# Numerators in like tiles, scaling one product later, and LayerNorm and weight parts moved, in an attention and MLP block

## The chip, the cores and the metric

The kernel runs on one core of a Trainium2 chip. The metric is the device time of one execution in microseconds (us). TensorE (PE, with its weight loads shown as PEld), VectorE (DVE), ScalarE (ACT), GpSimd (POOL) and SyncE (SP, which here only issues DMAs) each work through a queue of their own in order, and wait for one another by semaphores.

## The reference

A transformer block for 2048 tokens of width 640 with 32 heads of 20, all in fp32:

```
h = layernorm(x) * (1 + ca) + sa
pq, pk = per-head linear map of q and k
phi = concat(softmax(p), softmax(-p))        # for q and for k
kv  = phi_k^T v ;  z = sum over tokens of phi_k
o   = (phi_q kv) / (phi_q z + 1e-6)
x   = x + ga * (o @ wo)
h   = layernorm(x) * (1 + cb) + sb
x   = x + gb * (relu(h @ w1 + b1)^2 @ w2 + b2)
```

The six rows sa to gb come from silu(c) @ w_mod. The hidden width of the MLP is 1728.

## The kernel before

Precision: a large product is made of three fp32r products (high x high, high x low, low x high). A matrix is therefore kept as a high part, rounded to fp32r, and a low part, the rest. Small products are left in fp32, which TensorE does in two passes.

The work has three stages. The first (to about 262 us) makes k, v and q for 16 tiles of 128 tokens, the two softmaxes, and the sum kv over all tokens. The exponentials of q, "e", go to DRAM for tiles 0 to 11 and stay in SBUF for tiles 12 to 15. The second stage (about 262 to 409 us) is the one that the diff touches: it turns e into the output of the attention and multiplies by wo. The third is the MLP: a loop over eight blocks j of 256 tokens and seven steps n, with `up` (h @ w1) and `down` (@ w2).

The second stage, per tile t:

- `load_e(t)` (L772) brings e back from DRAM; its SBUF buffer must have been released by an earlier tile's scaling.
- `e_prod(t)` (L784): DVE multiplies e by z (L788) and sums over each head (L790). POOL then makes three small steps (L792, L794, L795), which give the denominator dd.
- `e_recip(t)` (L797): DVE takes the reciprocal (L801) and multiplies it by the softmax sums (L802), on DVE or POOL depending on the tile.
- `e_scale(t)` (L804): DVE scales e by that factor into one of four buffers "ezb" (L809 and a small piece, L814).

Per block j of two tiles: `tr_e(j)` (L820) transposes the scaled e on TensorE ("te", L829), and ACT copies it out (L831). `num(j)` (L835) makes the numerators: for five groups of six heads two products of 64 columns each, and for the last two heads one product with kv5, which holds their 40 columns three times side by side, so that the result has three copies on 120 partitions. The three tiles of the result are "numa", "numb" and "numc". `num_hi(j)` (L855): ACT rounds them to the high parts. `num_lo(j)` (L860): TensorE subtracts the high parts from the numerators by a product with minus the identity ("neg", L864), and ACT copies the rest out as low parts (L866). For the last two heads the 120 partitions end up as low, high, high against high, high, low rows of wo, so that one product does the work of three. `do_wo(j, i, h, a, b)` (L870) makes products a to b of the 16 that multiply tile i of the block by column part h (384 or 256 columns) of wo ("pwo"), and ACT copies the result out ("at", L884).

The loop over j runs from L1030; its body is an order written out by hand for PE, DVE, ACT and POOL. Iteration j multiplies block j by wo, transposes and makes the numerators of block j + 1, and does products and scalings for tiles b = 2j + 5, c = 2j + 6 and b - 1. SP is not part of the order by hand: its DMAs are placed by the framework's own planner. Within the loop also lie:

- `q_chain(t, False)` (the spread: maximum, minimum and two subtractions on DVE, L401 to L404), `exps` (two exponentials on ACT, L407 and L408) and `q_sums` (DVE, L449) for tiles 13, 14 and 15, whose softmax was left for later.
- `add_x` (L973) and `ln_parts` (L314) for block 0 of the MLP: the residual, then in three parts two sums, two squares and two scalings on ACT.
- `p_load`, `p_hi`, `p_lo` (L937 on): the next weight part of w1 or w2 is loaded, rounded by ACT to its high part (L916), and DVE makes its low part (L88). There are 28 parts in a fixed list. What is not made in the loop is made in the MLP, by `prep(4)` (one batch of four parts per step n of block 0; `PREPS`).

Of the kernel before, what the change touches and what calls it, by code (L numbers as in the profile page):

```python
# [11 lines left out]
AF = mybir.ActivationFunctionType  # L12
# [3 lines left out]
P = 128  # L16
# [35 lines left out]
def kernel(  # L52
# [23 lines left out]
    def mm(o, terms, first=True, last=True, skip=False):  # L76
        for i, (a, b) in enumerate(terms):
            nc.tensor.matmul(  # L78
                o, a, b,
                start=first and i == 0, stop=last and i == len(terms) - 1,  # L80
                skip_group_check=skip,
            )
# [323 lines left out]
    def exps(e):  # L406
        nc.scalar.activation(e[:, 0], e[:, 0], AF.Exp)  # L407
        nc.scalar.activation(e[:, 1], e[:, 1], AF.Exp, scale=-1.0)  # L408
# [363 lines left out]
    def load_e(t):  # L772
        if t >= KEPT:
            if t < NT:
                ET[t] = EQ[t]
            return
        ET[t] = tok2(("k", "k", f"x{t // 3 % 2}")[t % 3], f"el{t}")
        nc.sync.dma_start(flat(ET[t]), ESP[t])
# [5 lines left out]
    def e_prod(t):  # L784
        if t >= NT:
            return
        z = SCR[t % 2]
        nc.vector.tensor_tensor(z, flat(ET[t]), flat(zb), op=ALU.mult)  # L788
        dn = DN[t] = small([P, 2, H], "dn", f"dn{t}", 3)
        nc.vector.tensor_reduce(dn.rearrange("p s h -> p (s h)"), heads(z), axis=AX.X, op=ALU.add)  # L790
        rs = rs_q[:, t].rearrange("p (s h) -> p s h", s=2)
        nc.gpsimd.tensor_tensor(dn, dn, rs, op=ALU.mult)  # L792
        dd = DD[t] = small([P, H], "dd", f"dd{t}")
        nc.gpsimd.tensor_tensor(dd, dn[:, 0], dn[:, 1], op=ALU.add)  # L794
        nc.gpsimd.tensor_scalar(dd, dd, 1e-6, None, op0=ALU.add)  # L795

    def e_recip(t):  # L797
        if t >= NT:
            return
        rs = rs_q[:, t].rearrange("p (s h) -> p s h", s=2)  # L800
        nc.vector.reciprocal(DD[t], DD[t])  # L801
        (nc.vector if t < 6 or t == NT - 1 else nc.gpsimd).tensor_tensor(DN[t], rs, DD[t][:, None, :].to_broadcast([P, 2, H]), op=ALU.mult)  # L802

    def e_scale(t):  # L804
        if t >= NT:
            return
        dn = DN[t]
        EU[t] = EZB[t % 4]
        nc.vector.tensor_tensor(  # L809
            EU[t][:, :1200].rearrange("p (u s h d) -> p s u h d", s=2, h=3, d=DH),  # L810
            ET[t][:, :, :600].rearrange("p s (u h d) -> p s u h d", h=3, d=DH),
            dn[:, :, :30].rearrange("p s (u h) -> p s u h", h=3)[:, :, :, :, None].to_broadcast([P, 2, 10, 3, DH]), op=ALU.mult
        )
        nc.vector.tensor_tensor(  # L814
            EU[t][:, 1200:].rearrange("p (s h d) -> p s h d", s=2, d=DH),
            ET[t][:, :, 600:].rearrange("p s (h d) -> p s h d", d=DH),
            dn[:, :, 30:, None].to_broadcast([P, 2, 2, DH]), op=ALU.mult
        )
# [16 lines left out]
    def num(j):  # L835
        OT[j] = ht(f"ot{j}", j)
        ps = [bank(f"numa{j}"), bank(f"numb{j}"), tp(f"numc{j}")]
        for g in range(5):
            for c in range(2):
                mm(ps[g // 2][64 * c : 64 * c + 64, (g % 2) * 256 : (g % 2) * 256 + 256],  # L840
                   [(kvd[:, g, 64 * c : 64 * c + 64], EPT[j, g][:120, c])], first=(g % 2 == 0), last=False, skip=True)
        mm(ps[2][:120, 256:], [(kv5, EPT[j, 5][:80, 0])], first=False, last=False, skip=True)
        NUM[j] = ps
        OT[j, 5] = row("s3", f"ot5_{j}")[:, 80:336].bitcast(F32R)

# [2 lines left out]
    def num_parts(j):  # L848
        ps, parts = NUM[j], []
        for b, g in ((0, 2), (1, 2), (2, 1)):  # L850
            t = OT[j][:, 2 * b : 2 * b + g]
            parts.append((ps[b][:, : 256 * g].rearrange("p (g n) -> p g n", n=256), t[:, :, 0], t[:, :, 1]))
        return parts + [(ps[2][:120, 256:], OT[j, 5][:120], OT[j, 5][:120])]

    def num_hi(j):  # L855
        for b, (src, hi, _) in enumerate(num_parts(j)):
            r = GR[5][1] if b == 3 else P
            nc.scalar.activation(hi[:r], src[:r], AF.Copy)

    def num_lo(j):  # L860

        for b, (src, hi, low) in enumerate(num_parts(j)):
            r = GR[5][1] if b == 3 else P
            nc.tensor.matmul(src[:r], neg[:r, :r], hi[:r], start=False, stop=True, skip_group_check=True)  # L864
        for src, _, low in num_parts(j):
            nc.scalar.activation(low, src, AF.Copy)  # L866

    PWO, AT = {}, {}

    def do_wo(j, i, h, a=0, b=16):  # L870
        t = 2 * j + i
        if h == 0 and a == 0:
            PWO[t] = pj(f"pwo{t}")
            AT[t] = row("s2", f"at{t}")
        s = slice(i * P, (i + 1) * P)
        cs_, n = slice(*CUT[h]), CUT[h][1] - CUT[h][0]
        terms = []
        for g in range(5):
            w, o = WO[g], OT[j]
            terms += three(o[:, g, 0, s], o[:, g, 1, s], w[:, 0, cs_], w[:, 1, cs_])  # L880
        terms.append((OT[j, 5][:120, s], WO[5][:120, 0, cs_]))
        mm(PWO[t][h][:, :n], terms[a:b], first=(a == 0), last=(b == 16))
        if b == 16:
            nc.scalar.activation(AT[t][:, cs_], PWO[t][h][:, :n], AF.Copy)  # L884
            if h:
                nc.scalar.dma_start(A1[t], AT[t])
# [50 lines left out]
    def p_load(n=1):  # L937
        for _ in range(n):
            if todo["load"]:
                k, f = todo["load"].pop(0)  # L940
                prep_load(k, f, places[k, f](f"w{k}_{f}"))

    def p_hi(n=1):
        for _ in range(n):
            if todo["hi"]:
                prep_hi(*todo["hi"].pop(0))
# [69 lines left out]
    num(0)  # L1016
    num_hi(0)
    num_lo(0)
    e_recip(2)
    e_scale(2)  # L1020
    e_prod(3)
    e_recip(3)
    e_scale(3)
    e_prod(4)
    e_recip(4)
    load_e(5)
    load_e(6)
    SPREAD, SUMS = {1: 1, 3: 2}, {2: 1, 4: 2}
    ln0 = None
    for j in range(NB):  # L1030
        nxt = j + 1 < NB
        b, c = 2 * j + 5, 2 * j + 6
        late_te = j == 0
        te_at = (0, 1) if 0 < j < 6 else (1, 2)
        if j == 4:
            load_x1(0)
        if j < 5:
            p_load()
        if j == 5:
            q_chain(KEPT + 3, False)  # L1040
            e_scale(b - 1)
        else:
            e_prod(b)
            e_scale(b - 1)
            e_recip(b)
        load_e(b + 2)
        def te(at):
            for i, gs in enumerate((range(3), range(3, NG))):
                if nxt and not late_te and te_at[i] == at:
                    tr_e(j + 1, gs)  # L1050

        do_wo(j, 0, 0)
        te(0)
        do_wo(j, 0, 1)
        if j == 7:
            t2(0, 0)
            t2(0, 1)
        te(1)
        if j in SUMS:
            q_sums(KEPT + SUMS[j])  # L1060
        if j == 5:
            exps(EQ[KEPT + 3])
            q_sums(KEPT + 3)
            e_prod(b)
            e_recip(b)
        if j == 0:
            e_scale(b)
        e_prod(c)
        if j in SPREAD:
            q_chain(KEPT + SPREAD[j], False)  # L1070
        do_wo(j, 1, 0)
        if j == 7:
            t2(0, 2)
            t2(0, 3)
        te(2)
        if j == 6:
            next(ln0)
        if nxt:
            if late_te:
                tr_e(j + 1, range(NG))  # L1080
            num(j + 1)
            num_hi(j + 1)
        if j == 6:
            next(ln0)
        do_wo(j, 1, 1, 0, 8)
        if j == 7:
            t2(0, 4)
        if not nxt:
            do_wo(j, 1, 1, 8, 16)
        if nxt:  # L1090
            do_wo(j, 1, 1, 8, 11)
            num_lo(j + 1)
            do_wo(j, 1, 1, 11, 16)
        if j in SPREAD:
            exps(EQ[KEPT + SPREAD[j]])
        if j:
            e_scale(b)
        e_recip(c)
        load_e(c + 2)
        if j == 5:  # L1100
            add_x(0, 0, 1)
            ln0 = ln_parts(XM[0], "b0")
        if j == 6:
            next(ln0)
        if 1 <= j < 6:
            p_hi()
        if j == 5:
            p_load(2)
        if j == 6:
            p_hi(2)  # L1110
            p_lo(4)
            p_load(3)
        if j == 7:
            p_lo(3)
            p_load(2)
    order.__exit__(None, None, None)

# [447 lines left out]
```

## Time and profile before

| what | value |
|---|---|
| median of 3 runs | 801.46 us (798.03 to 801.79) |
| the profiled execution | 800.36 us, of which the span from first to last instruction is 798.7 us |
| PE, PEld, DVE, ACT, POOL busy | 98%, 94%, 73%, 56%, 16% of the span |
| attention stage, 262 to 409 us | PE busy 145.89 of 147 us, DVE 102.09, ACT 83.83, POOL 34.71 |
| HBM traffic over the span | 157 GB/s |

In a row of the timeline stand the start and the duration in us, the engine, the line, the operation, output <- input, the shape (rows x columns of the TensorE tile, then the moving data) and the count; in brackets the idle time of the engine ahead of it and what ended it. A row of several instructions lasts from the first one's start to the last one's end. In a row of waits stand the waiting engine and operation, what it waited for, and us in total, times, and the longest. In a row of groups stand busy us and mean ns of one, then idle us ahead of them. In a row of windows stand for PE, PEld, DVE, ACT and POOL busy us and instructions, then the granted TensorE clock, the share of the DMA engines and GB/s. "issue" is time in which the engine waited for nothing that the profile shows. TensorE's matmuls overlap: a matmul's duration reaches to the end of its pipeline, so the step from one to the next is shorter than its duration.

### The profile page before, as it was taken

Reading aid. Unit: us, or ns where it says so; the run is one execution under the profiler, and the core shown is the slowest. Engines: PE = TensorE matmul, PEld = TensorE weight load, DVE = VectorE, ACT = ScalarE, POOL = GpSimd, SP = SyncE. Lnnn points to the kernel's source line nnn. Section 1 sums busy time; section 2 is a strip of 40 time slices with the busy share of each in tenths; the row PEclk is TensorE's granted clock in tenths of the full one; section 3 lists DMA queues with packets and bytes.
Section 4 is the critical chain, followed back from the end, with each engine's and each line's share of the span. In section 5 each row is a group of like instructions: output and inputs, shape, how many; then the busy total and the mean of one; then the engine's idle time right before and its main releaser. Section 6 shows DMA issues by size and latency. Waiting matters only on the chain.

```text
span 798.7 us, 15281 instructions
## 1 busy us (share of the span) xinstructions
PE 785.4 (98%) x5983; PEld 750.5 (94%) x5983; DVE 579.3 (73%) x1046; ACT 443.3 (56%) x988; POOL 128.3 (16%) x259
## 2 busy tenths in 40 slices
PE   9999999999999999999999999998999999999997
PEld 8899999999999878898899999998999999999997
DVE  4499889998788688993546666775757667675756
ACT  4667675576753355565777737555364645536431
POOL 3001021010000114331000000131131313213110
PEclk9999999999999999999999999999999999999999
DMA  9713326423120243321347355996575967667450
GB/s 341 279 35 128 115 83 203 148 85 116 67 100 1 82 167 132 116 83 67 116 144 239 130 180 213 284 317 207 160 237 154 278 170 234 200 175 218 122 168 34
DMA packets 50560, 126.30 MB, mean 158 GB/s; under 512 B 5872, under 2 KB 6640, under 8 KB 50488
## 3 DMA queue, kind: packets, MB, share of 16 engines
q1 hardware_dynamic: 33432, 84.32, 31.0%
q0 software_dynamic: 14752, 35.76, 16.3%
q10 hardware_dynamic: 2304, 5.24, 1.7%
q8 instruction: 47, 0.77, 0.4%
q14 instruction: 25, 0.20, 0.1%
HBM read 95.32 MB, written 29.88 MB: 157 GB/s over the span
## 4 chain that ended last, share of the span: by engine, by line
PE 75%; DVE 10%; ACT 6%; issue 4%; POOL 3%; DMA 2%; POOLq 0%; ACTq 0%; DVEq 0%
PE up L78 18%; PE acc L78 14%; PE pk L78 8%; PE pq L78 7%; PE pv L78 7%; PE pwo L78 7%; PE acc3x L78 4%; PE kvp L421 2%; DVE dn L790 2%; DVE scr L788 2%; PE te L829 2%; DMA ring_b<-td_b 1%; PE ta L340 1%; PE tb L340 1%; DVE ezb L809 1%
## 5 line engine op out<-in xcount | busy, mean ns | idle before, releaser
L78 PE MATMUL up<-h,w 128*128 128x256 f32 x1640 | 208.7, 279 | 0.4 <-ACT ft L1149 0.4
L78 PEld LDWEIGHTS up<-h,w 128*128 128x128 f32 x1640 | 197.9, 189 | 1.1 <-ACT ft L1149 0.8
L1149 ACT ACTIVATE ft<-up,b_t 128x256 f32<-128x256 f32 x104 | 49.0, 472 | 106.6 <-PE up L78 106.1
L78 PE MATMUL acc<-w,ra 128*128 128x384 f32 x452 | 100.4, 338 | 0.4
L78 PE MATMUL pwo<-wo,ot 128*128 128x256 f32 (+3 forms) x512 | 83.2, 315 | 0.1
L1150 DVE TENSOR_TENSOR ft<-ft 128x256 f32<-128x256 f32 x104 | 44.0, 423 | 50.5 <-ACT ft L1149 48.8
L78 PE MATMUL pk<-wk,hT 128*128 128x384 f32 (+1 forms) x480 | 77.1, 312 | 0.9 <-ACT hT L352 0.9
L78 PEld LDWEIGHTS pwo<-wo,ot 128*128 128x128 f32 (+1 forms) x512 | 75.7, 188 | 1.9 <-ACT ot L866 0.4
L78 PEld LDWEIGHTS acc<-w,ra 128*128 128x128 f32 x452 | 72.7, 188 | 3.7 <-DVE ra L88 2.0
L78 PE MATMUL pq<-wq,hT 128*128 128x384 f32 (+1 forms) x480 | 74.9, 311 | 0.4 <-ACT k L397 0.4
L78 PE MATMUL pv<-wv,hT 128*128 128x384 f32 (+1 forms) x480 | 75.2, 309 | 0.0
L78 PEld LDWEIGHTS pk<-wk,hT 128*128 128x128 f32 x480 | 71.6, 188 | 2.7 <-ACT hT L352 1.1
L78 PEld LDWEIGHTS pq<-wq,hT 128*128 128x128 f32 x480 | 70.5, 188 | 1.5 <-ACT k L397 0.9
L78 PEld LDWEIGHTS pv<-wv,hT 128*128 128x128 f32 x480 | 70.5, 188 | 0.4
L88 DVE TENSOR_TENSOR ra<-ft,ra 128x384 fp32r<-128x384 f32 (+2 forms) x86 | 36.8, 449 | 34.3 <-ACT ra L1173 21.0
L88 DVE TENSOR_TENSOR h<-hfb,h 128x256 fp32r<-128x256 f32 x40 | 17.0, 425 | 46.4 <-ACT h L352 46.3
L1173 ACT ACTIVATE ra<-ft 128x384 fp32r<-128x384 f32 x48 | 25.2, 526 | 32.6 <-DVE ft L1150 25.2
L78 PE MATMUL acc3x<-w,ra 128*128 128x256 f32 x248 | 43.0, 281 | 0.0
L78 PEld LDWEIGHTS acc3x<-w,ra 128*128 128x128 f32 x248 | 39.5, 188 | 1.6 <-DVE y L1314 1.4
L1259 POOL DMA_DIRECT2D ring_a<-td_a x34 | 18.3, 540 | 129.9 <-PE acc L78 103.3
L792 POOL TENSOR_TENSOR dn<-dn,rs_q 128x64 f32<-128x64 f32 x16 | 14.0, 877 | 128.0 <-DVE dn L790 128.0
L1164 DVE TENSOR_TENSOR ft<-ft 128x128 f32<-128x128 f32 x136 | 33.3, 286 | 1.2
(241 smaller groups left out, 1424.5 us busy)
## 6 DMA issues: line engine op xcount, KB each, us to landing
ring_c<-td_c POOLq DMA_DIRECT2D x34, 384.0 KB, 4.6
ring_a<-td_a POOLq DMA_DIRECT2D x34, 384.0 KB, 4.2
ring_b<-td_b POOLq DMA_DIRECT2D x34, 256.0 KB, 4.5
esp<-eq SPq DMA_DIRECT2D x12, 640.0 KB, 3.0
el<-esp SPq DMA_DIRECT2D x12, 640.0 KB, 3.9
rw<-in_w SPq DMA_DIRECT2D x23, 320.0 KB, 3.1
wm<-in_w_mod SPq DMA_DIRECT2D x20, 320.0 KB, 3.8
xb<-in_x SPq DMA_DIRECT2D x8, 640.0 KB, 4.2
```

The source lines that it names most:

```text
L78: nc.tensor.matmul(o, a, b, start=first and i == 0, stop=last and i == len(terms) - 1, skip_group_check=skip,)
L88: (eng or nc.vector).tensor_tensor(out_lo, full, hi.bitcast(F32), op=ALU.subtract)
L340: nc.tensor.transpose(p[:, i * P : (i + 1) * P], xn[:, i, d * P : (d + 1) * P], ident)
L421: nc.tensor.matmul(kvp[64 * c : 64 * c + 64, g // 4, a : a + 2 * n].rearrange("p (s n) -> p s n", s=2), v[:, u], e[:, :, o : o + n], start ...
L788: nc.vector.tensor_tensor(z, flat(ET[t]), flat(zb), op=ALU.mult)
L790: nc.vector.tensor_reduce(dn.rearrange("p s h -> p (s h)"), heads(z), axis=AX.X, op=ALU.add)
L829: nc.tensor.transpose(p[:m, a : a + P], EU[2 * j + i][:, b : b + m], ident)
L1149: nc.scalar.activation(r, p, AF.Relu, bias=b1_t[:, f : f + 1])
L1150: nc.vector.tensor_tensor(r, r, r, op=ALU.mult)
L1164: nc.vector.tensor_tensor(t[:, o], t[:, a], t[:, b], op=op)
L1173: nc.scalar.activation(a[:, 0, :3], t[:, :3], AF.Copy)
L1259: nc.gpsimd.dma_start(RING[j, n, r], TD[n][r].bitcast(F32R))
```

## The change

The diff does five things:

- `e_recip`: the factor (L802) is always made on DVE.
- `num`: the product with kv5 is made in two halves, of 64 and 56 columns.
- `num_hi` and `num_lo`: the last part is rounded on all 120 partitions and subtracted with a 120x120 identity; only 40 partitions of the rest are copied out, so that the other 80 keep the high part.
- Ahead of the loop and in it, reciprocal and scaling of a tile stand behind the product of the next tile. For tile b the scaling moves from the end of an iteration (for j = 0, from before `e_prod(c)`) to the place behind `e_prod(c)` and ahead of the spread of a later tile; in j = 5 exps, sums and product of tile 15 come ahead of the second wo product.
- `add_x` and the three LayerNorm parts of the MLP's block 0 come earlier: from the end of j = 5 and three places in j = 6 to the start of j = 5, two places in j = 5 and one in j = 6. Of the weight parts, two more of the 28 are loaded, rounded and split in the loop (14 loads in place of 12, 9 of the others in place of 7).

```diff
--- before.py
+++ after.py
@@ -799,7 +799,7 @@
             return
         rs = rs_q[:, t].rearrange("p (s h) -> p s h", s=2)
         nc.vector.reciprocal(DD[t], DD[t])
-        (nc.vector if t < 6 or t == NT - 1 else nc.gpsimd).tensor_tensor(DN[t], rs, DD[t][:, None, :].to_broadcast([P, 2, H]), op=ALU.mult)
+        nc.vector.tensor_tensor(DN[t], rs, DD[t][:, None, :].to_broadcast([P, 2, H]), op=ALU.mult)
 
     def e_scale(t):
         if t >= NT:
@@ -839,7 +839,8 @@
             for c in range(2):
                 mm(ps[g // 2][64 * c : 64 * c + 64, (g % 2) * 256 : (g % 2) * 256 + 256],
                    [(kvd[:, g, 64 * c : 64 * c + 64], EPT[j, g][:120, c])], first=(g % 2 == 0), last=False, skip=True)
-        mm(ps[2][:120, 256:], [(kv5, EPT[j, 5][:80, 0])], first=False, last=False, skip=True)
+        for a, b in ((0, 64), (64, 120)):
+            mm(ps[2][a:b, 256:], [(kv5[:, a:b], EPT[j, 5][:80, 0])], first=False, last=False, skip=True)
         NUM[j] = ps
         OT[j, 5] = row("s3", f"ot5_{j}")[:, 80:336].bitcast(F32R)
 
@@ -853,17 +854,17 @@
         return parts + [(ps[2][:120, 256:], OT[j, 5][:120], OT[j, 5][:120])]
 
     def num_hi(j):
+        for src, hi, _ in num_parts(j):
+            nc.scalar.activation(hi, src, AF.Copy)
+
+    def num_lo(j):
+
         for b, (src, hi, _) in enumerate(num_parts(j)):
+            r = 120 if b == 3 else P
+            nc.tensor.matmul(src, neg[:r, :r], hi, start=False, stop=True, skip_group_check=True)
+        for b, (src, _, low) in enumerate(num_parts(j)):
             r = GR[5][1] if b == 3 else P
-            nc.scalar.activation(hi[:r], src[:r], AF.Copy)
-
-    def num_lo(j):
-
-        for b, (src, hi, low) in enumerate(num_parts(j)):
-            r = GR[5][1] if b == 3 else P
-            nc.tensor.matmul(src[:r], neg[:r, :r], hi[:r], start=False, stop=True, skip_group_check=True)
-        for src, _, low in num_parts(j):
-            nc.scalar.activation(low, src, AF.Copy)
+            nc.scalar.activation(low[:r], src[:r], AF.Copy)
 
     PWO, AT = {}, {}
 
@@ -1016,15 +1017,14 @@
     num(0)
     num_hi(0)
     num_lo(0)
+    e_prod(3)
     e_recip(2)
+    e_recip(3)
     e_scale(2)
-    e_prod(3)
-    e_recip(3)
+    load_e(5)
     e_scale(3)
+    load_e(6)
     e_prod(4)
-    e_recip(4)
-    load_e(5)
-    load_e(6)
     SPREAD, SUMS = {1: 1, 3: 2}, {2: 1, 4: 2}
     ln0 = None
     for j in range(NB):
@@ -1036,13 +1036,14 @@
             load_x1(0)
         if j < 5:
             p_load()
+        if j != 5:
+            e_prod(b)
+        e_recip(b - 1)
+        e_scale(b - 1)
         if j == 5:
             q_chain(KEPT + 3, False)
-            e_scale(b - 1)
-        else:
-            e_prod(b)
-            e_scale(b - 1)
-            e_recip(b)
+            add_x(0, 0, 1)
+            ln0 = ln_parts(XM[0], "b0")
         load_e(b + 2)
         def te(at):
             for i, gs in enumerate((range(3), range(3, NG))):
@@ -1051,21 +1052,22 @@
 
         do_wo(j, 0, 0)
         te(0)
+        if j == 5:
+            exps(EQ[KEPT + 3])
+            q_sums(KEPT + 3)
+            e_prod(b)
         do_wo(j, 0, 1)
         if j == 7:
             t2(0, 0)
             t2(0, 1)
         te(1)
+        if j == 5 or j == 6:
+            next(ln0)
         if j in SUMS:
             q_sums(KEPT + SUMS[j])
-        if j == 5:
-            exps(EQ[KEPT + 3])
-            q_sums(KEPT + 3)
-            e_prod(b)
-            e_recip(b)
-        if j == 0:
-            e_scale(b)
         e_prod(c)
+        e_recip(b)
+        e_scale(b)
         if j in SPREAD:
             q_chain(KEPT + SPREAD[j], False)
         do_wo(j, 1, 0)
@@ -1073,15 +1075,11 @@
             t2(0, 2)
             t2(0, 3)
         te(2)
-        if j == 6:
-            next(ln0)
         if nxt:
             if late_te:
                 tr_e(j + 1, range(NG))
             num(j + 1)
             num_hi(j + 1)
-        if j == 6:
-            next(ln0)
         do_wo(j, 1, 1, 0, 8)
         if j == 7:
             t2(0, 4)
@@ -1093,25 +1091,19 @@
             do_wo(j, 1, 1, 11, 16)
         if j in SPREAD:
             exps(EQ[KEPT + SPREAD[j]])
-        if j:
-            e_scale(b)
-        e_recip(c)
         load_e(c + 2)
         if j == 5:
-            add_x(0, 0, 1)
-            ln0 = ln_parts(XM[0], "b0")
-        if j == 6:
             next(ln0)
         if 1 <= j < 6:
             p_hi()
         if j == 5:
-            p_load(2)
+            p_lo(4)
+            p_load(4)
         if j == 6:
-            p_hi(2)
-            p_lo(4)
+            p_hi(4)
+            p_lo(5)
             p_load(3)
         if j == 7:
-            p_lo(3)
             p_load(2)
     order.__exit__(None, None, None)
```

## The prediction

> **What bounds the kernel now.** I read the page's busy times first, then the waits of the weight-load queue (PEld) over the whole run, then those waits one by one in the timeline.
>
> ```profile
> PE 785.4 (98%) x5983; PEld 750.5 (94%) x5983; DVE 579.3 (73%) x1046; ACT 443.3 (56%) x988; POOL 128.3 (16%) x259
> PEld acc L78 <- DMA ring_b<-td_b: 2.4, 1, 2.4
> PEld numc L864 <- issue: 1.8, 7, 0.3
> PEld acc L78 <- DVE w L88: 1.5, 4, 0.4
> PEld te L829 <- DVE ezb L809: 0.7, 1, 0.7
> PEld pwo L78 <- ACT ot L866: 0.4, 1, 0.4
> ```
>
> TensorE is busy for 98% of the span. A faster DVE, ACT or POOL is worth nothing by itself; the change can gain only where TensorE stands still, or where it does the same work in less time. The waits name the places (us in total, times, longest). They are small, a few us of 800, so the question is which of these rows the diff touches.
>
> **Part 1: the subtraction of the rounded numerators (num_lo).** Before, heads 30 and 31 are subtracted by a 40x40 matmul between 128x128 ones; after, by a 120x120 one.
>
> ```profile
> 301.78 0.39 PE L864 MATMUL numb<-ot,neg 128*128 128x512 f32 x1
> 302.01 0.52 PE L864 MATMUL numc<-ot,neg 128*128 128x256 f32 x2
> 302.45 0.51 PE L78 MATMUL pwo<-wo,ot 128*128 128x256 f32 x2
> 302.22 0.11 PEld L864 LDWEIGHTS numc<-ot,neg 40*40 40x40 f32 x1 [0.25 <-issue]
> 307.17 2.13 PE L78 MATMUL pwo<-wo,ot 128*128 128x256 f32 x16
> ```
>
> In the last row 16 products of 256 columns take 2.13 us. One alone shows about 0.28 (the end of its pipeline included), so they follow each other every (2.13 - 0.28) / 15 = 0.12 us. A 512-column one takes 0.23 (301.78 to 302.01). Undisturbed, the two numc products at 302.01 would hand over to pwo at 302.01 + 0.12 + 0.12 = 302.25. In fact the 40x40 weights wait 0.25 although every input is there, and the two pwo products last 0.51 where 0.28 + 0.12 = 0.40 is usual: the first truly begins at 302.45 + 0.11 = 302.56. That is 0.31 to 0.32 us late. There are eight numerators, one ahead of the loop and seven in it: **8 x 0.32 = 2.6 us** gone, if a 120x120 tile follows a 128x128 one without a pause, as 128x120 transposes follow 128x128 products. ACT does not pay: the rounding of this part grows from 40 to 120 partitions and the last copy shrinks from 120 to 40, at the same 256 columns.
>
> **Part 2: the last numerator (num), in halves of 64 and 56 columns.**
>
> ```profile
> 298.96 0.36 PEld L78 LDWEIGHTS numc<-ept,kvd 120*64 120x64 f32 x4
> 299.71 0.28 PEld L78 LDWEIGHTS numc<-ept,kvd 80*120 80x120 f32 x2 [0.38 <-issue]
> 298.31 1.03 PE L78 MATMUL numb<-ept,kvd 120*64 120x256 f32 x8
> 261.73 1.38 PE L421 MATMUL kvp<-ek,vt 128*64 128x120 f32 x22 [0.27 <-ACT vt L390]
> 263.04 1.14 PE L78 MATMUL pq<-wq,hT 128*128 128x384 f32 x5
> 303.68 2.42 PE L78 MATMUL pwo<-wo,ot 128*128 128x384 f32 x13
> ```
>
> The 64-column products run in pairs: eight last 1.03, one of them 0.38 to its end, so a pair takes (1.03 - 0.38) / 3 = 0.22. The 120-column product takes two passes of about that length behind a pause of 0.38 in the loads. Split, it is two pairs, 2 x 0.22: the same streaming time, with four loads instead of two, hidden like those of the other pairs. What becomes of the pause? It looks like 8 x 0.38 = 3.1 us to be had. But look where 64-column products (kvp) hand over to 128-column ones (pq, 263.04): the five pq rows last 1.14, while at the step of pwo's 384 columns ((2.42 - 0.34) / 12 = 0.17) they should last 0.34 + 4 x 0.17 = 1.03. There is a pause of 0.1 at least there too. So I expect it to move from ahead of the last numerator to ahead of pwo. Bounds: nothing to 3.1 gained; I take **0**, the kvp row being the nearest. The Trainium skill, page "TensorEngine Tiling (Array Packing)", section Key Properties, says that a change of the tiling mode, as against the tile, drains TensorE. By it one drain per numerator stays, wherever it is put, and the gain here is 0 too; the kvp row agrees. Only ahead of the loop, where TensorE waits for ACT's rounding of numc, does the earlier end of the product count: **0.2 us**, once, an estimate from half of the 0.38.
>
> **Part 3: reciprocal and scaling one product later.** Per tile DVE does a product (L788, L790), a reciprocal with its factor (L801, L802) and a scaling (L809 and a small second piece). The grouped rows are those of 262 to 428 us:
>
> ```profile
> L788 DVE TENSOR_TENSOR scr<-el,zb 128x1280 f32<-128x1280 f32 x12 | 17.5, 1460 | 0.0
> L790 DVE TENSOR_REDUCE dn<-scr 128x64 f32<-128x1280 f32 x16 | 23.8, 1486 | 0.6
> L809 DVE TENSOR_TENSOR ezb<-el,dn 128x1200 f32<-128x1200 f32 x12 | 16.9, 1407 | 0.2
> L801 DVE RECIPROCAL dd<-dd 128x32 f32<-128x32 f32 x16 | 5.6, 352 | 10.3 <-POOL dd L795 10.3
> L802 DVE TENSOR_TENSOR dn<-rs_q,dd 128x64 f32<-128x64 f32 x7 | 1.6, 225 | 0.2
> 282.02 1.49 DVE L790 TENSOR_REDUCE dn<-scr 128x64 f32<-128x1280 f32 x1
> 284.66 0.35 DVE L801 RECIPROCAL dd<-dd 128x32 f32<-128x32 f32 x1 [1.15 <-POOL dd L795]
> 305.94 1.25 PE L829 MATMUL te<-ident,ezb 128*120 128x128 f32 x10
> 317.87 0.81 DVE L401 TENSOR_REDUCE mxq<-eq 128x32 f32<-128x640 f32 x1
> 321.05 1.40 DVE L809 TENSOR_TENSOR ezb<-el,dn 128x1200 f32<-128x1200 f32 x1
> 322.50 0.63 PEld L829 LDWEIGHTS te<-ident,ezb 128*120 128x120 f32 x6 [0.73 <-DVE ezb L809]
> 321.16 0.74 ACT L407 ACTIVATE eq<-eq 128x640 f32<-128x640 f32 x1 [1.57 <-DVE eq L404]
> ```
>
> DVE stands still for 10.3 us in all ahead of reciprocals, because POOL's three small steps need 1.15 behind a sum. With a product of 2.9 us put between sum and reciprocal, these waits go, but for tile 3's ahead of the loop and tile 15's, which has no product behind it. The nine factors that move from POOL (tiles 6 to 14) cost DVE 9 x 0.225 = 2.0. Little of this lies on TensorE's path. One place does: tile 7 is scaled at 321.05, behind the spread of tile 13 (317.87 to 321.05, 3.2), and transposes wait 0.73 for it at 322.50. After, tile 7 is scaled ahead of that spread.
>
> Is anything else late then? I follow DVE from tile 2's sum, which ends at 283.5: product 3 (2.9), factors 2 and 3 with one wait (1.8), scalings 2 and 3 (3.0), products 4 and 5 (5.8), factor and scaling 4 (2.1), product 6 (2.9), factor and scaling 5 (2.1): 304.1. Then product 7, scaling 6, product 8, scaling 7 (10.0): 314.1, and the spread: 317.3. Tile 5 is needed by the transposes of 305.94, which come 0.8 earlier by parts 1 and 2, at 305.1: 1.0 to spare, the tightest place. Tile 7 has 6 to spare, and the exps of tile 13, on which ACT waited until 321.16, wait no more. So **0.7 us** is gained. The loads of e follow the release of their buffers, tile by tile; it comes earlier by the same list, so that none is later. The spread of tile 13, now behind a scaling, would cost ACT 2.1 if DVE had no lead; the list has it ready 1.9 ahead of 319.6, when ACT began to wait.
>
> **Part 4: LayerNorm and weight parts.**
>
> ```profile
> 396.50 0.83 ACT L325 ACTIVATE junkb<-xm,smb 128x640 f32<-128x640 f32 x1
> 398.29 0.57 ACT L866 ACTIVATE ot<-numa 128x512 fp32r<-128x512 f32 x1
> 398.92 0.82 PEld L78 LDWEIGHTS pwo<-wo,ot 128*128 128x128 f32 x5 [0.43 <-ACT ot L866]
> L331 ACT ACTIVATE xm<-xm,nbb,sqb 128x640 f32<-128x640 f32 x2 | 1.7, 916 | 0.5 <-ACT at L884 0.5
> 391.45 0.49 ACT L884 ACTIVATE at<-pwo 128x384 f32<-128x384 f32 x1 [1.82 <-PE pwo L78]
> 416.26 0.30 PEld L78 LDWEIGHTS acc<-w,ra 128*128 128x128 f32 x2 [0.39 <-DVE w L88]
> 379.08 1.49 DVE L449 TENSOR_REDUCE rs_q<-eq 128x64 f32<-128x1280 f32 x1 [12.71 <-ACT eq L408]
> 405.72 0.43 DVE L88 TENSOR_TENSOR h<-hfb,h 128x256 fp32r<-128x256 f32 x1 [13.94 <-ACT h L352]
> L916 ACT ACTIVATE w<-rw 128x640 fp32r<-128x640 f32 x11 | 7.4, 725 | 0.4 <-ACT at L884 0.4
> L88 DVE TENSOR_TENSOR w<-rw,w 128x640 fp32r<-128x640 f32 x11 | 8.3, 819 | 0.1
> ```
>
> In j = 6 the two squares (from 396.50) hold ACT until 398.29, so the low parts of the numerators come late and pwo waits 0.43. After, the squares stand at the end of j = 5, and the scaling of x (1.7 us) fills the hole of 1.82 ahead of 391.45. **0.4 us** gained. In j = 5 the two sums take the place of two exps of like length, and the exps go forward to where DVE's spread is long done (12.7 us of idle DVE lay there): nothing.
>
> The four waits for w (1.5 in all) are down products of the MLP that need an odd chunk of w2. It is the first of a batch of four weight parts, prepared by ACT and DVE just ahead of its use. With two parts more made in the attention loop every batch shifts by two, and that chunk becomes the third of the batch before. **1.5 us** gained. The price, two roundings (2 x 0.73) and two low parts (2 x 0.82) more in j = 5 and 6, and four loads issued there by SP instead of two, falls where DVE idles for 12.7 and 13.9 us and ACT loses nothing: one scaling of x goes from that place. Without that cover it would be 3.1 us.
>
> **The sum:** 2.6 + 0.2 + 0.7 + 0.4 + 1.5 = **5.4 us**. The profiled execution took 800.36 (span 798.7), so 795.0. The median of the runs is 801.46 (798.03 to 801.79); the profiled one lies among them, and I stay with it.
>
> **The rivals.**
> - *The halves do not overlap* (56 columns not paired with 64): two passes more per numerator, 8 x 2 x 0.22 = 3.5, give 798.5. For it: no row here has a 56-column tile. Against it: all 64-column products pair. 0.10.
> - *The waits come back elsewhere*: scalings, squares and batches only trade places, parts 3 and 4 give nothing, and 800.36 - 2.8 = 797.6 is left. For it: tile 5's 1.0 us is thin. Against it: tile 7's 6. 0.14.
> - *More goes*: the pause of part 2 vanishes, 795.0 - 3.1 = 791.9, or the ring wait below does not occur, 790.8. For it: 798.03 was seen for the same kernel. 0.12.
> - *The ring fetches, slower than before.*
>
> ```profile
> 500.00:545.00 45.00, 42.20 (x311) 41.15 (x311) 30.20 (x78) 22.26 (x50) 10.43 (x20) 0.96 0.95 302
> ```
>
> For these 45 us the DMA engines are 95% busy, and one late ring_b costs 2.4 and a stretch at a lower clock (granted 0.96 of 45 us: 1.8), 4.2 in all. SP's order is not written by hand; with the loads and stores of x1 and w moved it may come out otherwise, and stores of td fall behind other transfers. Each further such wait costs 4.2; from two on (5.4 / 4.2 = 1.3) the kernel is slower: 803.4. Against it: what the diff moves lies over 70 us before. The Trainium skill, page "TensorE: Matmul & The Clock Gate", Part 1, puts the idle time that halves the clock at about 3.4 us; by it a wait of 2.4 costs 2.4 alone, and this rival would end at 799.8. The lowered clock in the row behind a wait of 2.4 speaks against that, and the measurement decides. 0.07.
>
> **How the numbers follow.** Forecast 795.0, own range 793.5 to 797, chance 0.57. A measurement of this kernel tells about 0.5%, 4 us, from no change, so faster means below 796.4: 0.50 of the forecast's 0.57 and the third rival's 0.12, 0.62. Within lie the forecast's other 0.07, the first two rivals (0.24) and 0.03 of the ring's: 0.34. Beyond 804.4 lies 0.04, for rings that wait more than twice. The range of 791 to 799 leaves out the ring's 0.07 and about half of the third rival.
>
> **What would show it.** No 40x40 form and no "numc L864 <- issue" (part 1). A late first pwo behind num, none ahead of the split product, steps of 0.22 for its pairs (part 2). No te wait for ezb past 300, a wait ahead of the reciprocals of tiles 3 and 15 only (part 3). No "pwo <- ACT ot L866", no "acc <- DVE w" (part 4). I am wrong if the 56-column half runs alone, if te waits near 305, if the 120x120 tile also drains the array, or if the ring waits change.

## The result and the profile after

| | before | after |
|---|---|---|
| median (us) | 798.03 (9 runs, 796.93 to 801.79) | 793.43 (9 runs, 791.36 to 796.49) |
| profiled execution (us) | 800.36, span 798.7 | 793.69, span 792.0 |

The ratio is 0.994, with a 95% interval of 0.9926 to 0.9954: faster by 4.6 us by the medians, 3.7 to 5.9 by the interval. The forecast was 795.0 in a range of 791 to 799; the narrower range of 793.5 to 797, which had a chance of 0.57, was just missed. The busy times and the largest waits of the weight-load queue over the whole run, after (us in total, times, longest):

```profile
PE 779.7 (98%) x5999; PEld 747.6 (94%) x5999; DVE 581.8 (73%) x1055; ACT 442.6 (56%) x988; POOL 123.0 (16%) x250
PEld acc L78 <- DVE ra L88: 2.8, 10, 0.3
PEld acc L78 <- issue: 2.8, 1, 2.8
PEld pwo L78 <- issue: 2.7, 7, 0.4
```

Of the five waits that the prediction began with four are gone: no numc without a releaser in the subtraction, no te behind ezb, no pwo behind ot, no acc behind w. The fifth, the ring's wait for ring_b, has shrunk to 0.2, and the 2.8 without a releaser stands in its place. But two rows stand higher: pwo now waits 0.4 seven times, and acc waits for ra, the split activations of the MLP, ten times in place of eight (2.8 us in place of 2.0).

To say where the time came from I measure two stretches on TensorE. The **attention stretch** runs from the first numerator (numa, about 282.7) to the last transposition of h (tb x2, about 404 to 408). **Block 0** runs from there to the next tb x4, one block of the MLP later. Matmuls before:

```profile
282.69 1.08 PE L78 MATMUL numa<-ept,kvd 120*64 120x256 f32 x8
407.90 0.38 PE L340 MATMUL tb<-ident,xm 128*128 128x128 f32 x2
446.00 0.60 PE L340 MATMUL tb<-ident,xm 128*128 128x128 f32 x4
```

And after:

```profile
282.82 1.08 PE L78 MATMUL numa<-ept,kvd 120*64 120x256 f32 x8
403.83 0.38 PE L340 MATMUL tb<-ident,xm 128*128 128x128 f32 x2
441.09 0.60 PE L340 MATMUL tb<-ident,xm 128*128 128x128 f32 x4
```

The attention stretch went from 407.90 - 282.69 = 125.21 to 121.01: **4.20 gained**. Block 0 went from 38.10 to 37.26, but three traces with the old MLP (e1 to e3 below) also have 37.26 to 37.48 there, and two more with the new one (e7, e8) have 37.01 and 37.78, so that no gain of the change in it is clear of this scatter. The first stage differs by 0.13. The rest of the 6.67 us between the two profiled executions is the lowered clock behind the ring of before. Stretches of 5 and 45 us, of before and then of after (the last three columns are granted clock, DMA share, GB/s):

```profile
540.00:545.00 5.00, 3.80 (x19) 3.80 (x20) 0.29 (x1) 1.84 (x2) 0.53 (x1) 0.66 0.94 308
```

```profile
495.00:540.00 45.00, 42.39 (x323) 41.42 (x322) 30.81 (x80) 23.11 (x52) 10.18 (x20) 1.00 0.95 303
```

An estimate of what the lowered clock cost is 5 x (1 - 0.66) = 1.7, and 4.20 + 0.84 - 0.13 + 1.7 = 6.6. None of the other traces shows a granted clock below 1.00 around the ring. It belongs to this one execution, which is 2.3 above the median of nine.

### The profile page after: what moved, and what is told of

The parts are those of the page before. It is cut to its first block, busy times and chain, and to the rows that moved or that the text cites. A ratio compares the mean times of both kernels' runs of the same rounds, so it can differ in the third digit from the quotient of the medians.

```text
span 792.0 us, 15313 instructions
## 1 busy us (share of the span) xinstructions
PE 779.7 (98%) x5999; PEld 747.6 (94%) x5999; DVE 581.8 (73%) x1055; ACT 442.6 (56%) x988; POOL 123.0 (16%) x250
## 4 chain that ended last, share of the span: by engine, by line
PE 81%; ACT 5%; DVE 5%; DMA 4%; issue 2%; POOL 1%; SPq 0%; ACTq 0%; POOLq 0%; DVEq 0%
PE up L78 19%; PE acc L78 14%; PE pwo L78 10%; PE pk L78 8%; PE pq L78 7%; PE pv L78 7%; PE acc3x L78 4%; PE kvp L421 2%; PE te L829 2%; DMA ring_a<-td_a 1%; PE numa L78 1%; PE tb L340 1%; PE ta L340 1%; PE numc L78 1%; PE numb L78 1%
## 5 line engine op out<-in xcount | busy, mean ns | idle before, releaser
L78 PE MATMUL pwo<-wo,ot 128*128 128x256 f32 (+3 forms) x512 | 81.1, 311 | 0.0
L351 ACT ACTIVATE hfb<-tb,cols_b 128x256 f32<-128x256 f32 x40 | 22.5, 562 | 18.4 <-PE tb L340 10.8
```

The source lines that it names most:

```text
L78: nc.tensor.matmul(o, a, b, start=first and i == 0, stop=last and i == len(terms) - 1, skip_group_check=skip,)
L351: nc.scalar.activation(hf, p[:, :256], AF.Identity, bias=cols[:, d : d + 1], scale=cols[:, 5 + d : 6 + d])
```

## The experiments

The theory was that of the prediction: five parts with a gain of their own each. The first five kernels do one part alone; three more take up single steps; the last four follow up what the first ones left open. Each is compared with before, run beside it (medians of 797.91 to 798.34 there). The stretches are worked out as above, from the same three rows of each trace:

| kernel | median, us | ratio to before (95%) | attention stretch | block 0 |
|---|---|---|---|---|
| before | 798.03 | | 125.21 | 38.10 |
| after | 793.43 | 0.994 (0.9926 to 0.9954) | 121.01 | 37.26 |
| e1_neg120 | 796.71 | 0.9987 (0.9976 to 0.9999) | 124.19 | 37.27 |
| e2_split | 797.24 | 0.9995 (0.9985 to 1.0004) | 125.11 | 37.26 |
| e3_order | 797.00 | 0.9993 (0.9977 to 1.0009) | 124.50 | 37.48 |
| e4_norm | 798.43 | 1.0009 (0.9998 to 1.0019) | 126.21 | 36.93 |
| e5_weights | 800.26 | 1.0031 (1.0018 to 1.0043) | 125.08 | 39.37 |
| e6_twos | 795.66 | 0.9981 (0.9967 to 0.9995) | 121.05 | 41.11 |
| e7_r64 | 795.39 | 0.9964 (0.9953 to 0.9976) | 123.86 | 37.01 |
| e8_r80 | 793.59 | 0.9947 (0.9929 to 0.9965) | 121.12 | 37.78 |
| e9_half_late | 792.36 | 0.9923 (0.9908 to 0.9937) | 121.09 | 36.52 |
| e10_sum_later | 791.85 | 0.9917 (0.99 to 0.9935) | 121.08 | 35.78 |
| e11_both | 792.53 | 0.9922 (0.9905 to 0.994) | 121.09 | 35.78 |
| e12_no_weights | 793.9 | 0.994 (0.9922 to 0.9957) | 121.04 | 37.00 |

The attention stretch repeats to 0.1 us (121.01 to 121.12) in the seven kernels whose attention is that of after, or differs from it only in the 80 rows of e8 or the weight parts of e12; the medians have intervals of 1.5 to 3 us. So where the two differ, single steps of the attention are read from the stretch. Block 0 scatters more, by up to 0.8 us between kernels of the same MLP code; why, comes with e9. What is said of it below rests on the waits as well.

**The subtraction on 120x120, alone** (before, with this edit):

```diff
-        for b, (src, hi, low) in enumerate(num_parts(j)):
+        for b, (src, hi, _) in enumerate(num_parts(j)):
+            r = 120 if b == 3 else P
+            nc.tensor.matmul(src, neg[:r, :r], hi, start=False, stop=True, skip_group_check=True)
+        for b, (src, _, low) in enumerate(num_parts(j)):
             r = GR[5][1] if b == 3 else P
...
-            nc.tensor.matmul(src[:r], neg[:r, :r], hi[:r], start=False, stop=True, skip_group_check=True)
-        for src, _, low in num_parts(j):
-            nc.scalar.activation(low, src, AF.Copy)
+            nc.scalar.activation(low[:r], src[:r], AF.Copy)
```

> The kernel before with the 120x120 subtraction alone. Theory (a product of another tile size makes the array stop twice, 0.32 us per numerator): 2.6 us less, no idle time ahead of the numc weights in the subtraction, and each turn of the loop 0.32 shorter; the te wait of 0.7 and the four waits for w stay. Rival (the stop belongs to what follows, and moves to pwo): less than 0.5 us.

The stretch gains 1.02, not 2.6. Two waits of the weight loads grew, and a third of 0.37 (te for ezb, at 387.85) is new. The two in the timeline of e1_neg120:

```profile
324.06 1.07 PEld L829 LDWEIGHTS te<-ident,ezb 128*120 128x120 f32 x10 [1.85 <-DVE ezb L809]
...
399.45 2.57 PEld L78 LDWEIGHTS pwo<-wo,ot 128*128 128x128 f32 x15 [0.80 <-ACT ot L866]
```

They were 0.73 and 0.43 before, so the three took back 1.12 + 0.37 + 0.37 = 1.9 of what the subtraction saved. DVE and ACT finish the scaled tile and the low parts when they always did; TensorE, earlier, waits longer for them. What is saved between two such meetings is handed over only if the other engine is moved too.

**The subtraction at other sizes** (after, with this edit; 64 in e7_r64, 80 in e8_r80):

```diff
-            r = 120 if b == 3 else P
-            nc.tensor.matmul(src, neg[:r, :r], hi, start=False, stop=True, skip_group_check=True)
+            r = 64 if b == 3 else P
+            nc.tensor.matmul(src[:r], neg[:r, :r], hi[:r], start=False, stop=True, skip_group_check=True)
```

> The changed kernel with the last subtraction on 64 rows and columns in place of 120 (the rows above 40 are not read later). Theory (a tile of at most 64 rows and columns puts the array in another mode and makes it stop): the 0.32 us per numerator come back, 2.6 us more. Rival (a tile of odd size, like 40, was the trouble): no change.

> The changed kernel with the last subtraction on 80 rows and columns in place of 120. Theory (above 64 it is the same mode as 128): no change, no idle time ahead of it. Rival (any tile smaller than its neighbours costs): 2.6 us more.

The weight loads of the last subtraction in e7_r64, then in e8_r80:

```profile
302.40 0.13 PEld L864 LDWEIGHTS numc<-ot,neg 64*64 64x64 f32 x1 [0.25 <-issue]
```

```profile
301.51 0.38 PEld L864 LDWEIGHTS numc<-ot,neg 128*128 128x128 f32 x2
```

At 64x64 the load stands alone and waits 0.25 for nothing, as the 40x40 one did. At 80x80 it joins the 128x128 row without a wait. The stretch is 123.86 against 121.12: 2.74, or 0.34 for each of eight numerators. With DVE and ACT moved, the subtraction is worth what its rows promised. So it is the form of the tile that costs, and not that it is smaller than its neighbours.

**The last numerator in halves, alone:**

```diff
-        mm(ps[2][:120, 256:], [(kv5, EPT[j, 5][:80, 0])], first=False, last=False, skip=True)
+        for a, b in ((0, 64), (64, 120)):
+            mm(ps[2][a:b, 256:], [(kv5[:, a:b], EPT[j, 5][:80, 0])], first=False, last=False, skip=True)
```

> The kernel before with the last numerator in halves of 64 and 56 columns alone. Theory (the stop moves from ahead of the last numerator to ahead of pwo): 0.0 to 0.2 us less, with 0.2 of late start at pwo behind num. Rival 1 (the stop vanishes): 1.5 to 3 us less. Rival 2 (the halves do not pair): 3.5 us more.

Nothing: 0.10 in the stretch, a ratio of 0.9995 (0.9985 to 1.0004). The matmuls after, around one numerator:

```profile
298.68 1.04 PE L78 MATMUL numc<-ept,kvd 120*64 120x256 f32 x8
299.65 1.57 PE L78 MATMUL pwo<-wo,ot 128*128 128x256 f32 x11
```

The weight loads of the same place, after:

```profile
298.47 0.79 PEld L78 LDWEIGHTS numc<-ept,kvd 120*64 120x64 f32 x8
299.65 1.36 PEld L78 LDWEIGHTS pwo<-wo,ot 128*128 128x128 f32 x11 [0.39 <-issue]
```

Eight products last 1.04, the two halves paired among them like the others (numb: 1.03 for eight). The pause of 0.38 ahead of the 120-column product is now 0.39 ahead of pwo. The waits of e2_split (288 to 409 us) have it seven times, in the same 2.7 us in all as after:

```profile
PEld pwo L78 <- issue: 2.7, 7, 0.4
PEld numc L865 <- issue: 1.7, 7, 0.3
```

Ahead of the loop the earlier end of the product does count, as forecast: from the first numa to the numc weights of the subtraction it takes 286.43 - 282.69 = 3.74 before and 3.55 in e2_split, 0.2 less. But in e2_split the one wait of te for ezb grew from 0.73 to 1.08.

**Reciprocal and scaling one product later, alone** (its core; the loop is reordered in the same manner):

```diff
-        (nc.vector if t < 6 or t == NT - 1 else nc.gpsimd).tensor_tensor(DN[t], rs, DD[t][:, None, :].to_broadcast([P, 2, H]), op=ALU.mult)
+        nc.vector.tensor_tensor(DN[t], rs, DD[t][:, None, :].to_broadcast([P, 2, H]), op=ALU.mult)
...
         e_prod(c)
+        e_recip(b)
+        e_scale(b)
...
-        if j:
-            e_scale(b)
-        e_recip(c)
```

> The kernel before with the new places of product, reciprocal and scaling alone, and the factor always on DVE. Theory: only the one wait of te for ezb goes, 0.7 us less, all of it in the third turn of the loop, while DVE's 10.3 us of waiting ahead of reciprocals shrink to about 2. Rival (DVE's place matters in every turn): 2 us less or more.

The stretch gains 0.71, and te waits for ezb nowhere in it. The grouped row of the reciprocals shows what DVE got back. It is the row of after (262 to 425 us); e3_order has the same 1.8 of waiting:

```profile
L801 DVE RECIPROCAL dd<-dd 128x32 f32<-128x32 f32 x16 | 5.5, 346 | 1.8 <-POOL dd L795 1.8
```

10.3 us of idle DVE are 1.8, and TensorE received 0.7 of it.

**The places of LayerNorm, alone:**

```diff
+            add_x(0, 0, 1)
+            ln0 = ln_parts(XM[0], "b0")
...
+        if j == 5 or j == 6:
+            next(ln0)
...
-            add_x(0, 0, 1)
-            ln0 = ln_parts(XM[0], "b0")
-        if j == 6:
```

> The kernel before with the LayerNorm parts alone at their new places. Theory: pwo's wait for ACT in the last turn goes (0.4 us), and with ACT free earlier the wait of up for h at the start of the MLP too (0.3): 0.7 us less in all. Rival (the wait for h belongs to the weight parts that moved): 0.4 us less, and the wait for h stays.

The stretch is 1.00 longer. ACT in e4_norm, turn j = 5:

```profile
377.67 0.72 ACT L320 ACTIVATE sameb<-xm 128x640 f32<-128x640 f32 x1
...
379.11 0.72 ACT L407 ACTIVATE eq<-eq 128x640 f32<-128x640 f32 x1
...
380.74 0.58 ACT L858 ACTIVATE ot<-numa 128x512 fp32r<-128x512 f32 x1
```

Its weight loads:

```profile
381.37 0.19 PEld L864 LDWEIGHTS numa<-ot,neg 128*128 128x128 f32 x1 [0.58 <-ACT ot L858]
381.85 0.19 PEld L864 LDWEIGHTS numb<-ot,neg 128*128 128x128 f32 x1 [0.30 <-ACT ot L858]
382.39 0.42 PEld L864 LDWEIGHTS numc<-ot,neg 128*128 128x128 f32 x2 [0.35 <-ACT ot L858]
```

The two sums are in front of the rounding while the two exps are still there, and the subtraction waits 1.23. Only the new order of part 3 takes the exps away; after has none of these waits in that turn. At the other end, pwo's wait is gone, and block 0 is about 0.3 shorter (36.93): the wait of its first up product for h, 0.27 before, is gone, since the scaling is done a turn earlier. The weight parts do not remove it: e5_weights still has it (0.26), e12_no_weights has not.

**The weight parts, alone, and all but them:**

```diff
         if j == 5:
-            p_load(2)
-        if j == 6:
-            p_hi(2)
...
+            p_load(4)
+        if j == 6:
+            p_hi(4)
+            p_lo(5)
```

> The kernel before with the weight parts alone at their new places. Prediction on record: the four waits for w go, 1.5 us less. What the profile after suggests: the waits for w go, but waits for ra of 0.3 to 0.4 take their place in the next steps, and 0.5 us is left; the wait for h at the start of the MLP goes too if it belongs to these parts (0.3 more).

> The changed kernel with the weight parts at their old places. Prediction on record: 1.5 us slower than the changed kernel. What the traces now suggest: the four waits for w come back (1.4 us in all), and the waits for ra that stand in their place (1.5 us) go: within 0.5 us of the changed kernel, on either side. The wait of up for h at the start of the MLP stays away if the LayerNorm parts removed it.

Alone they make the kernel slower, 1.0031 (1.0018 to 1.0043); block 0 of e5_weights has a wait of 1.17 for ra behind ACT and one of 0.60 of up for ACT's hfb (the transposed x, copied out for h), which before has not. Taken out of after, they change nothing: 0.994 both ways, and block 0 is 37.00 without them, 37.26 with them. Waits of 400 to 460 us, in e12_no_weights and then in after:

```profile
PEld acc L78 <- DVE w L88: 1.0, 3, 0.4
PEld acc L78 <- DVE ra L88: 0.3, 1, 0.3
```

```profile
PEld acc L78 <- DVE ra L88: 1.2, 4, 0.3
PEld acc L78 <- ACT ra L1165: 0.4, 1, 0.4
```

The waits for w are gone, as forecast, and as much waiting for ra stands in their place. What makes ra late? My first theory was the batch of four low parts on DVE (3.03 us) ahead of it. The test halves the batches (after, with this edit):

```diff
-    PREPS = iter([0, 4] * 5 + [0, 1])
+    PREPS = iter([2, 2] * 5)
```

> The changed kernel with the MLP's weight parts made two and two, at both places of a step, and not four at one. Theory A (four lows on DVE and four roundings on ACT hold up the square, the sum of x and the split that the next down product waits for): the waits for ra of steps 2, 3 and 5 of block 0 shrink, 0.7 to 1.2 us less. Rival B (the chain from up through square and split to down is itself longer than the products that cover it): the waits stay, no change.

**That theory fell.** Block 0 grew to 41.11. The waits of e6_twos (400 to 460) are longer than in after:

```profile
PEld acc L78 <- ACT ra L1165: 2.8, 4, 1.8
PEld acc L78 <- DVE ra L88: 1.2, 4, 0.3
```

ACT in e6_twos shows why, first for the two waits of 0.30 for ACT's part of ra:

```profile
415.06 0.74 ACT L1375 ACTIVATE xx<-xm 128x640 f32<-128x640 f32 x1 [1.71 <-DVE xm L976]
...
415.80 1.35 ACT L917 ACTIVATE w<-rw 128x640 fp32r<-128x640 f32 x2
417.06 0.46 ACT L1141 ACTIVATE ft<-up,b_t 128x256 f32<-128x256 f32 x1
```

ACT works in order: the sum of the next LayerNorm (L1375) waits 1.71 for x + attention (xm, L976), and behind it stand two roundings and only then ft, the output of up, which is squared and then split. (The wait of 0.48 of step 1 has the two roundings ahead of ft, without a sum.) The longest wait, 1.75, has another cause: ACT waits 2.69 for the load of a weight part from DRAM, the one of the second cause below, and ft stands behind that too. ACT, then TensorE's weight load:

```profile
433.24 0.74 ACT L917 ACTIVATE w<-rw 128x640 fp32r<-128x640 f32 x1 [2.69 <-DMA rw<-in_w]
```

```profile
435.45 0.30 PEld L78 LDWEIGHTS acc<-w,ra 128*128 128x128 f32 x2 [1.75 <-ACT ra L1165]
```

The waits are 2.4 us more than in after. The rest of the 3.85 by which block 0 grew is about what a lowered clock behind the 1.75 costs (last section), by an estimate 5 x (1 - 0.72) + 5 x (1 - 0.94) = 1.7. The chain of the sum in after, in order, as the timeline has it on DVE, ACT and the weight loads:

```profile
410.97 3.03 DVE L88 TENSOR_TENSOR w<-rw,w 128x640 fp32r<-128x640 f32 x4
...
413.92 0.42 DVE L1142 TENSOR_TENSOR ft<-ft 128x256 f32<-128x256 f32 x1
...
414.26 0.82 DVE L976 TENSOR_TENSOR xm<-xm,xx 128x640 f32<-128x640 f32 x1
...
415.11 0.74 ACT L1375 ACTIVATE xx<-xm 128x640 f32<-128x640 f32 x1 [1.93 <-DVE xm L976]
...
415.85 0.46 ACT L1141 ACTIVATE ft<-up,b_t 128x256 f32<-128x256 f32 x1
...
417.36 0.76 DVE L88 TENSOR_TENSOR ra<-ft,ra 128x384 fp32r<-128x384 f32 x2 [0.59 <-ACT ra L1165]
...
417.97 0.19 PEld L78 LDWEIGHTS acc<-w,ra 128*128 128x128 f32 x1 [0.30 <-DVE ra L88]
```

Four low parts, a square, the sum's input, the sum, ft, its square and the split: from 410.97 to 417.97 without room. The next four low parts begin at 418.18, 7.2 after the first; TensorE's own two steps, from the down product at 410.17 to the one at 417.38, would take 6.9 without the wait of 0.30. When the wait for w went, this chain became the last to arrive. A second cause shows later in the same block. On ACT, after:

```profile
428.22 0.18 ACT L1380 ACTIVATION_READ_ACCUMULATOR xx<-xm,smb 128x1 f32 x1
...
433.57 2.00 ACT L917 ACTIVATE w<-rw 128x640 fp32r<-128x640 f32 x3 [2.14 <-DMA rw<-in_w]
```

ACT waits 2.14 for the load of chunk 13 of w1, the half-width one. Its raw copy goes to the buffers "s2" and not to "s1", as those of the full chunks do, and LayerNorm's two squares (L1380) hold both buffers of "s2"; the first ends at 428.40. The waits of SP in after (420 to 434) show the load behind them:

```profile
SPq L907 <- ACT xx L1380: 0.3, 1, 0.3
```

```profile
428.95 0.42 SPq L907 DMA_DIRECT2D rw<-in_w  x1
```

The load is issued at 428.95, behind three others in SP's queue; in e7_r64 and e10_sum_later it is issued within 0.03 us of the first square's end. With the parts two places earlier in the list, ACT wants it before it can have come: it waits 1.9 to 3.3 for it in e5, e7, e8 and after (3.26 in e5_weights), and 0.7 to 2.3 with the old list.

This load also goes with the scatter of block 0. In the old MLP ACT waits 0.69 (e2), 0.95 (e1), 1.62 (e3) and 2.25 (before) for it, and block 0 takes 37.26, 37.27, 37.48 and 38.10; in the new one the waits are 1.88 (e7), 2.14 (after) and 2.65 (e8), with 37.01, 37.26 and 37.78. Before has two waits of TensorE at the end of block 0 that e1 and e2 lack, 0.30 for ra (444.11) and 0.38 for w (445.20): 0.7 of the 0.84 by which its block 0 is longer than theirs. Why the load comes later in one execution than in another, the runs do not show.

Two edits of after try one cause each, and a third both:

```diff
+    preps.remove(("1", 13))
+    preps.insert(25, ("1", 13))
...
-    LN_AT0 = {"load": 0, "add": (2, 4), "ln": (2, 4, 6, 6, 8, 8), 10: (0, 1), 11: (2, 3), 12: (4,)}
+    LN_AT0 = {"load": 0, "add": (2, 4), "ln": (3, 5, 6, 6, 8, 8), 10: (0, 1), 11: (2, 3), 12: (4,)}
```

> The changed kernel with the half-width part of w1 (chunk 13) three places later in the list of weight parts. Theory (its raw copy must wait for a buffer that the LayerNorm squares of block 1 release in step 3; two places earlier in the list, ACT waits 2.1 us for that load in step 4 and the split for step 5 is late): ACT's wait for the load goes, and the 0.7 us of waits for ra ahead of step 5's down products shrink to 0.25 or nothing: 0.4 to 0.7 us less. Rival (the wait in step 5 is the same chain as in steps 2 and 3): no change.

> The changed kernel with the sums of block 1's LayerNorm at the end of steps 1 and 2, behind the split, and not in their middle. Theory (ACT stands at the sum until DVE has made four lows, a square and the addition; the evacuation of up and the split behind it are late, and this and not the weights bounds steps 2 and 3): the waits for ra at the down products of steps 2 and 3 go, 2 x 0.37 = 0.7 us less; that of step 1 stays. Rival (the four lows themselves hold the chain): the waits stay.

> The changed kernel with both edits, the half-width part later and the sums behind the split. Theory: the two gains add, 1.1 to 1.4 us less than the changed kernel, and of block 0's waits for ra only those of step 1 are left. Rival: they share one cause and give no more than the better of the two.

The waits of 400 to 460 us, in e9_half_late (chunk 13 later) and then in e10_sum_later (the sum behind the split):

```profile
PEld acc L78 <- DVE ra L88: 0.9, 3, 0.3
```

```profile
PEld acc L78 <- DVE ra L88: 0.3, 1, 0.3
```

e9 removes the waits of the step that the late load held, 0.40 and 0.30: block 0 is 0.74 shorter than after. e10 removes those of the two steps whose split stood behind the sum, as forecast, and e9's as well: 1.48 shorter. ACT still waits for the half-width load there, but only 1.04, and no split is late behind it; whether the moved sum or the scatter of the load did that is not shown. ACT in e10_sum_later shows the split free of the sum:

```profile
414.57 0.47 ACT L1141 ACTIVATE ft<-up,b_t 128x256 f32<-128x256 f32 x1 [0.96 <-PE up L78]
...
419.85 0.72 ACT L1375 ACTIVATE xx<-xm 128x640 f32<-128x640 f32 x1
```

ft now waits for TensorE instead of being waited for. Both edits together give e10's 35.78 and no more. With the sum moved as well, block 0 is 37.00 - 35.78 = 1.2 shorter than without the weight parts, near the 1.5 forecast; but what the moved sum gives without them was not run, so that the 1.2 belongs to the pair. e10_sum_later has the lowest median, 791.85, 0.9917 (0.99 to 0.9935); that interval overlaps after's, and the 1.5 us between them are read from block 0.

## Why the prediction came out as it did

- **Part 1, 2.6: right** once DVE and ACT had moved: 2.74 between 64x64 and 80x80 in the changed kernel, and no wait with 120x120; alone it gave 1.02. The third doubt, that a 120x120 tile would also drain the array, is answered.
- **Part 2, nothing: right,** and for its reason: the pause went from the split product to pwo. The 56-column half runs in a pair with the 64-column one. The pause ahead of pwo is 0.39, where the kvp row had suggested 0.1 at least. The 0.2 ahead of the loop is there (0.19 in e2_split). The upper bound, 8 x 0.38, is 3.0 and not 3.1; only a rival's 791.9 rests on it.
- **Part 3, 0.7: right,** 0.71 in e3_order, and te did not wait for tile 5 after. The list of DVE's work held: tile 5 was scaled by 304.4 (304.1 by the list) and tile 7 by 314.6 (314.1). The lead over ACT that the same list gives is 319.6 - 317.3 = 2.3, not 1.9, which changes nothing. What the prediction did not say is that part 1 depends on parts 3 and 4: the 2.6 were there only because DVE and ACT moved with TensorE.
- **Part 4, LayerNorm, 0.4: right** for pwo, with a further 0.3 not foreseen, the wait of up for h. "The exps go forward [...]: nothing" holds only together with part 3; without it the subtraction waits 1.2 and the stretch is 1.0 longer.
- **Part 4, weight parts, 1.5: the step that failed.** That the chunk "becomes the third of the batch before", with 1.5 gained, is true in its first half: the waits for w are gone. But I asked where else the added instructions might collide in the attention loop, and not what arrives next at the products that no longer wait for w. The split of ra arrived 0.3 to 0.4 later than they could have begun, and the shifted list met a busy buffer. Measured against e12_no_weights, block 0 is 0.3 longer (37.26 against 37.00), and by the scatter of its kernels between nothing and 0.8 longer: no gain.
- **The sum.** 5.4 forecast; 4.6 by the medians (3.7 to 5.9). The four terms of the attention stretch make 3.9, and it gained 4.2; the 1.5 of block 0 did not come.
- **The starting point** was the other error. I stayed with the profiled 800.36, between runs of 798.03 and 801.79. Nine runs put before at 798.03. The excess carried its mark: the granted clock of 0.96 in the row that I quoted for a rival. 798.03 - 5.4 would have been 792.6. So the forecast's 795.0 against 793.43 is 2.3 too much start less 0.8 too much gain. That the two errors pull in opposite directions is luck; with either alone the forecast would still have had the measured time in its range.
- **The rivals.** "The waits come back elsewhere" occurred in part, in the MLP instead of the attention. The halves overlap. The ring made nothing slower: every trace waits about 1.3 to 2.8 at it, before and after alike.

The five parts alone move the medians by -1.0, -0.4, -0.6, +0.7 and +2.5 us (their ratios less 1, of 798), +1.2 in all; together by -4.6. In the attention stretch, where the scatter is small, they give 1.02 + 0.10 + 0.71 - 1.00 + 0.13 = 0.96 alone and 4.20 together.

## What to carry to other kernels

A wait that is removed is worth, at the most, the distance to the next arrival at the same instruction, so follow that chain (here low parts, sum, split) before booking the gain. Where several engines meet once per turn, a saving on one is handed over only if the others move too, and parts tried singly can each look useless or harmful. Before a forecast stands on one execution, look for what only that one has: a stretch at a lower clock is such a thing.

## What the hardware showed that I had not expected

**How long TensorE stands does not by itself decide about its clock.** In before a wait of 2.4 us, which ended at 541.20, came with a granted clock of 0.66 over the 5 us from 540. After has a longer wait at the same ring:

```profile
534.56 0.47 PEld L78 LDWEIGHTS acc<-ring_a,rs 128*128 128x128 f32 x3 [2.77 <-issue]
```

The granted clock was 1.00 in the 45 us around it, and it was 1.00 around a wait of 2.69 in e3_order too. In e6_twos a wait of 1.75, which ended at 435.45, came with 0.72 in the same 5 us:

```profile
435.00:440.00 5.00, 4.55 (x23) 4.26 (x24) 3.16 (x6) 5.00 (x9) 0.00 (x0) 0.72 0.36 117
```

What else decides, the runs do not show; the several shorter waits near that of e6_twos may count. The prediction weighed a figure of about 3.4 us of idle time (the Trainium skill, page "TensorE: Matmul & The Clock Gate", Part 1); waits of 2.4 and 1.75 came with a lowered clock here, and waits of 2.77 and 2.69 did not, so the measurement speaks against reading that figure as the length of one wait.
